# A transformer block on one core: attention scores from two float32r pieces in 48 rows, two heads on the two halves of the array's rows, all maxima from PSUM

## The chip, the core and the metric

The kernel runs on one core of a Trainium2 chip. A core has a matrix engine (TensorE; PE in the profile, PEld for its weight loads), VectorE (DVE), ScalarE (ACT), GpSimd (POOL), and SyncE (SP), which only issues DMAs here. Matrix products go to PSUM, of which the kernel uses eight banks of 512 float32 a partition; DVE and ACT read it; everything else lies in SBUF on 128 partitions. The metric is the time of one execution in microseconds of the device, the median of several runs.

## The reference

One block over 2048 tokens of 512 features, in float32, with 32 heads of 16 features and a feed-forward width of 1792:

```python
mod = (_silu(c) @ w_mod).reshape(c.shape[0], 6, 1, -1)
sa, ca, ga, sb, cb, gb = (mod[:, 0], mod[:, 1], mod[:, 2], mod[:, 3], mod[:, 4], mod[:, 5])
h = _layernorm(x) * (1 + ca) + sa
q, k, v = (h @ wqkv) by head
scores = jnp.einsum("bhqd,bhkd->bhqk", q, k) * Dh ** -0.5
o = jnp.einsum("bhqk,bhkd->bhqd", softmax(scores), v)
x = x + ga * (o @ wo)
h = _layernorm(x) * (1 + cb) + sb
x = x + gb * (_gelu(h @ w1 + b1) @ w2 + b2)
```

The inputs are scaled so that scores are large: the softmax needs the maximum of each row of scores, to float32 accuracy.

## The kernel before, in words

The program has three stages: the projections to q, k and v (with the first layer norm), attention, and the output projection with the feed-forward. The order of instructions on each engine is the order in which the code issues them (a manual schedule); the framework adds the semaphore waits.

Attention works in 32 **units**: a group of four heads (`g`, eight of them) by a block of 512 queries (`qb`, four). A unit has 16 **steps** (`s`), one for each chunk of 128 keys. The scores stand transposed, keys on the partitions and queries in the free dimension.

A score needs float32 accuracy. q and k are split in three bf16 pieces each (in `proj_qk`; ACT, DVE, ACT and POOL make them), and written to DRAM. `build` loads them from there into two stacks, `qst` and `kst`, by 12 DMAs for a group: six products of pieces times 16 features are 96 rows, so that one bf16 matmul gives a float32 score. For three heads of a unit three more rows hold the negative maximum of the query, again in three pieces, against rows of ones in `kst` (99 rows). Their maxima are found ahead: `max_pair` computes scores with the queries on the partitions, 2 x 512 keys into two PSUM banks (`bank_mx`, two such buffers), and DVE takes the maximum of the 1024 (L355, L357), 24 pairs a unit, 34 pairs ahead of the attention at its start (24 and `AHEAD`). `max_rows` joins them, transposes them on PE (L369), copies (L371), splits on POOL (L374, L376), and two DMAs bring them under the queries.

The unit's first head has it otherwise. Its raw scores are computed with a lead of `LEAD` = 20 steps (`raw_chunk`, L393), copied by ACT to a ring of 22 SBUF tiles (L395), and DVE keeps their running maximum (L400). When the unit's 16 chunks are there, `raw_max` transposes the maximum and reduces it (L406, L408), and `raw_spread` sends it to DRAM and back to all partitions (L412 and L414, tiles `x` and `rmaxb`). POOL subtracts it from each tile of the ring (`raw_shift`, L418), and ACT exponentiates in place (L757).

In a step PE computes three scores into a PSUM tile `sc` each (L735, `bank`, three buffers of a bank), ACT exponentiates each (L737), a raw chunk is taken, and parts of the maximum pairs stand between the heads (1.5 pairs a step). Behind them stand the products with v of the step before (`pv_step`, L564): four float32 matmuls of 32 columns each, one for each head, on four quarters of the array's columns. Each float32 matmul is two passes in the trace. The unit's sums gather in one PSUM bank `pv`; at the unit's end ACT copies it (`attn_out`, L550) and eight DMAs store it. The last unit has no maxima to look for; two of its heads then share a wide exponential (L742, L744), and the output projection of the first block stands between its steps (L668).

PSUM: four banks for `mx`, three for `sc`, one for `pv`. Matmuls of the projections and of the feed-forward have float32r operands (128 rows, 512 columns; L286, L668, L809). Pairs and raw chunks that are needed first stand between the matmuls of the last projections (`fill`).

Of the kernel before, what the change touches and what calls it, by code (L numbers as in the profile page):

```python
# [31 lines left out]
RS = 22  # L32
LEAD = RS - 2
# [9 lines left out]
def block_kernel(ctx: ExitStack, tc: tile.TileContext, x, wqkv, wo, w1, b1, w2, b2, c, w_mod, out):  # L43
# [13 lines left out]
    ps_sc = ctx.enter_context(tc.tile_pool(name="ps_sc", bufs=3, space=PSUM))  # L57
# [4 lines left out]

    def bank():
        return ps_sc.tile([P, TB], F32, tag="sc", name="sc")
# [4 lines left out]
    # Rows (part, head in the chunk x d, token); the parts are the three bf16 pieces of a float32.  # L69
    qk_d = [[dram.tile([3, P, S], BF, name=f"qk{w}{k}") for k in range(4)] for w in range(2)]  # L70
# [23 lines left out]
    scm, stx = pool("stx")  # L94

    def stacks(pl):
        return [pl.tile([P, 4, S], BF, name=n) for n in ("qst", "kst")]

    st_x = stacks(stx)
    # The stacks of the even groups lend their space to other data before the first and after the last of them.  # L100
    space = [t.bitcast(F32) for t in st_x]
    halves = [[sp[:, :, :D], sp[:, :, D:]] for sp in space]

# [12 lines left out]
    ones = vwpool.tile([3, S], BF, name="ones")  # L116
# [57 lines left out]
    # silu(c) = c / (1 + exp(-c))  # L174
# [25 lines left out]
    def mod_cols(v, r):  # L200
        """modc[:, v, chunk]: 1 + scale and shift of the feature on the partition"""
# [22 lines left out]
    def ln_stats(tiles):  # L224
        """mean and (var + eps) ** -0.5 of the rows of four tiles"""
# [7 lines left out]
    def transposed(xn, hi, lo, v, pl, bk, engs):  # L233
        """hi + lo of (xn ** T) * (1 + scale) + shift, by feature chunk"""
# [24 lines left out]
    def mx_halves():  # L259
        """the chunks' banks, two to a tile"""  # L260
# [19 lines left out]
    def mm3(ps, ahi, alo, bhi, blo, fill=(), late_b=True):  # L280
        """the three products of a = ahi + alo and b = bhi + blo (alo * blo is below float32's own rounding)"""
# [8 lines left out]
    def proj_qk(b, k, w, fill=()):  # L290
# [32 lines left out]
    st = {}  # L323

    def build(g, t0=0, t1=S):
        q, k = st[g]
        r0 = (g % 2) * 64

        def src(w, parts):
            ap = qk_d[w][g // 2][:, r0 : r0 + 64, t0:t1]  # L330
            return [ap[p].rearrange("(j d) t -> d j t", d=DH) for p in parts]

        for w, dst, parts in ((1, k, (0, 0, 0, 1, 1, 2)), (0, q, (0, 1, 2, 0, 1, 0))):
            for i, ap in enumerate(src(w, parts)):
                sy.dma_start(dst[i * DH : (i + 1) * DH, :, t0:t1], ap)

    def one_rows(k):
        sy.dma_start(k[96:99], one_d[:, None, :].to_broadcast([3, 4, S]))
# [109 lines left out]
    for b in range(NB):  # L448
# [13 lines left out]
        if b == NB - 1:  # L462
            build(0, b * TB, S)
# [446 lines left out]
```

## Time and profile before

| what | us |
|---|---|
| runs: median (lowest to highest, 3 runs) | 2304.33 (2303.45 to 2307.96) |
| span of the profiled execution | 2265.9 |
| first and last pv matmul (the attention stage) | 205.0 and 1905.8 |
| PE busy, share of the span | 2034.7, 90% |
| DVE busy | 1756.7, 78% |
| ACT busy | 1507.4, 67% |
| POOL busy | 1014.6, 45% |
| mean granted TensorE clock, share of full | 0.925 |

The span goes from the first to the last instruction of one profiled execution; the runs' time includes what lies around it. Shares of busy time are means over stages with different limits, and a matmul's recorded time includes its way through the array, so that the starts of two matmuls show what one of them takes in a row. A group of instructions is shown with its source line, engine, operation, tiles, form, count, busy time in all, mean time of one in ns, and the idle time before it with what ended it. A row of a stretch of time is explained where it is shown.

### The profile page before, as it was taken

What the parts mean: (1) busy time and instruction counts of PE and PEld (TensorE: products, weight loads), DVE (VectorE), ACT (ScalarE), POOL (GpSimd) and SP (SyncE); (2) the same over time, 40 slices, a digit from 0 to 9 for tenths busy, and PEclk for the clock granted to TensorE, in tenths of its full rate; (3) what the DMA queues carried; (4) which work ended last, traced back from release to release, by engine and by line L of the source; (5) the groups of instructions that cost most, each with busy time, mean ns of one, the idle gap of its engine ahead of it and who ended that gap; (6) DMA issues with size and microseconds to landing.
All of it is one profiled execution on the core that took longest, in us unless ns stands there. A gap on an engine that the chain in (4) does not pass through costs nothing.

```text
span 2265.9 us, 28250 instructions
## 1 busy us (share of the span) xinstructions
PE 2034.7 (90%) x10202; PEld 855.5 (38%) x10202; DVE 1756.7 (78%) x1819; ACT 1507.4 (67%) x2818; POOL 1014.6 (45%) x890
## 2 busy tenths in 40 slices
PE   8999888888888888888888998888888879999999
PEld 6764222222222222222222222222222224778887
DVE  5288888888888888888888888888888856873653
ACT  3346877777777877777777888777877776222222
POOL 3335454444444444444444444444444554554553
PEclk9999998998888999888889999989999989999999
DMA  6746200400050005001300310050000122532431
GB/s 232 185 152 115 38 18 13 76 8 8 8 76 8 13 8 78 8 8 34 50 8 8 57 27 8 8 76 8 8 13 9 48 81 74 167 116 75 118 115 56
DMA packets 115777, 125.70 MB, mean 55 GB/s; under 512 B 29305, under 2 KB 80537, under 8 KB 115636
## 3 DMA queue, kind: packets, MB, share of 16 engines
q1 hardware_dynamic: 115636, 123.89, 23.5%
q8 instruction: 80, 1.31, 0.3%
q14 instruction: 61, 0.50, 0.1%
HBM read 96.54 MB, written 27.31 MB: 55 GB/s over the span
## 4 chain that ended last, share of the span: by engine, by line
PE 55%; DMA 20%; DVE 12%; issue 4%; ACT 3%; POOL 3%; SPq 0%; ACTq 0%; POOLq 0%; DVEq 0%
PE pv L564 15%; DMA x<-rmax 13%; PE sc L735 10%; PE mx L355 9%; PE sc L286 9%; DMA rmaxb<-x 6%; DVE racc L400 6%; PE mx L809 4%; DVE mxp L357 4%; PE sc L393 3%; POOL ring L418 2%; PE sc L668 2%; PE pv L809 1%; ACT p L737 1%; PE sc L406 1%
## 5 line engine op out<-in xcount | busy, mean ns | idle before, releaser
L357 DVE TENSOR_REDUCE mxp<-mx 128x1 f32<-128x1024 f32 x768 | 921.1, 1218 | 98.2 <-PE mx L355 83.8
L737 ACT ACTIVATE p<-sc 128x512 f32<-128x512 f32 x1488 | 794.5, 598 | 231.2 <-PE sc L735 209.2
L418 POOL TENSOR_TENSOR ring<-ring,rmaxb 128x512 f32<-128x512 f32 x512 | 693.8, 1388 | 479.3 <-DMA rmaxb<-x 479.3
L355 PE MATMUL mx<-kst,qst 96*128 96x512 bf16 x1536 | 621.4, 408 | 1.2 <-DVE mxp L357 1.2
L400 DVE TENSOR_TENSOR racc<-racc,ring 128x512 f32<-128x512 f32 x448 | 509.8, 1138 | 138.4 <-ACT ring L395 137.5
L735 PE MATMUL sc<-qst,kst 99*128 99x512 bf16 x1488 | 609.1, 411 | 6.6 <-DVE r L298 5.5
L564 PE MATMUL pv<-ring,vg 128*32 128x512 f32 x1024 | 577.1, 647 | 10.6 <-ACT osb L550 9.4
L564 PE MATMUL pv<-p,vg 128*32 128x512 f32 x3072 | 583.7, 647 | 0.0
L757 ACT ACTIVATE ring<-ring 128x512 f32<-128x512 f32 x512 | 331.1, 647 | 108.1 <-POOL ring L418 107.9
L735 PEld LDWEIGHTS <-kst 99*128 99x128 bf16 x1488 | 152.4, 103 | 538.9 <-issue 435.3
L395 ACT ACTIVATE ring<-sc 128x512 f32<-128x512 f32 x492 | 301.9, 614 | 12.0 <-PE sc L393 12.0
L393 PE MATMUL sc<-qst,kst 96*128 96x512 bf16 x492 | 199.7, 406 | 99.8 <-ACT p L737 99.6
L374 POOL CAST m<-mr 12x128 bf16<-12x128 f32 x96 | 27.5, 287 | 420.5 <-DVE mr L371 416.4
L355 PEld LDWEIGHTS <-qst 96*128 96x128 bf16 x1536 | 155.8, 103 | 155.4 <-issue 51.6
L564 PEld LDWEIGHTS pv<-ring,vg 128*32 128x32 f32 x1024 | 73.0, 111 | 355.5 <-issue 339.6
L787 ACT ACTIVATE g<-sc,b_c 128x512 f32<-128x512 f32 x56 | 38.6, 690 | 240.4 <-PE sc L286 236.3
L600 POOL TENSOR_TENSOR w1l<-w1r,w1h 128x512 fp32r<-128x512 f32 x56 | 76.7, 1369 | 151.2 <-DVE w1h L599 135.6
L791 DVE TENSOR_TENSOR glo<-g,ghi 128x512 fp32r<-128x512 f32 x56 | 59.3, 1058 | 98.1 <-ACT ghi L790 98.0
L406 PE MATMUL sc<-ident,racc 128*128 128x128 f32 x128 | 28.8, 367 | 95.1 <-DVE racc L400 95.1
L602 POOL TENSOR_TENSOR w2l<-w2r,w2h 128x512 fp32r<-128x512 f32 x56 | 81.2, 1450 | 6.5 <-DVE w2h L601 6.1
L393 PEld LDWEIGHTS <-kst 96*128 96x128 bf16 x512 | 52.7, 103 | 74.7 <-issue 22.9
L564 PEld LDWEIGHTS pv<-p,vg 128*32 128x32 f32 x3072 | 79.8, 111 | 0.0
(145 smaller groups left out, 1898.6 us busy)
## 6 DMA issues: line engine op xcount, KB each, us to landing
w1r<-in_B_w_dram SPq DMA_DIRECT2D x56, 256.0 KB
w2r<-in_B_w_dram SPq DMA_DIRECT2D x56, 256.0 KB
qk<-parts SPq DMA_DIRECT2D x32, 384.0 KB
kst<-qk SPq DMA_DIRECT2D x42, 256.0 KB
qst<-qk SPq DMA_DIRECT2D x42, 256.0 KB
rmaxb<-x SPq DMA_DIRECT2D x32, 256.0 KB
kst<-in_w_mod_dram SPq DMA_DIRECT2D x6, 1024.0 KB
v<-vst SPq DMA_DIRECT2D x8, 664.0 KB
```

Source lines behind the costliest of these rows:

```text
L286: te.matmul(ps, p, q, start=i == 0, stop=i == len(terms) - 1)
L355: ms.append(lambda s=s, k0=k0: te.matmul(ps[:, s], q[:96, j, q0 : q0 + P], k[:96, j, k0 : k0 + TB], start=True, stop=True))
L357: red = lambda: ve.tensor_reduce(mxp[u][:, i : i + 1], ps, axis=AX.XY, op=ALU.max, negate=True)
L393: te.matmul(ps, k[:96, 0, kc * P : (kc + 1) * P], q[:96, 0, qb * TB : (qb + 1) * TB], start=True, stop=True)
L395: ac.activation(sl, ps, AF.Copy)
L400: ve.tensor_tensor(r_acc[u], r_acc[u], sl, op=ALU.max)
L418: gp.tensor_tensor(sl, sl, r_max[c // NKC], op=ALU.subtract)
L564: te.matmul(cur_pv[0][32 * j : 32 * (j + 1)], vg[g][:, kc, j * VW : j * VW + 32], p[:, j - 1] if j else ring[s % RS], start=kc == 0, stop= ...
L735: te.matmul(ps, k[:99, j, kc * P : (kc + 1) * P], q[:99, j, qb * TB : (qb + 1) * TB], start=True, stop=True)
L737: ac.activation(p[:, j - 1], ps, AF.Exp, scale=SCALE)
L757: ac.activation(sl, sl, AF.Exp, scale=SCALE)
L809: te.matmul(acc[qb][t], p[:, sl], q, start=f == 0 and n == 0, stop=f == NF - 1 and n == 2)
```

## The change

q and k are now split in two float32r pieces each (ACT makes the first, DVE the second). Three products of pieces (high x high, low x high, high x low) times 16 features are 48 rows, and two rows more hold the two pieces of the negative maximum against ones: 50 rows (`KR`, `KX`). Two heads of a unit stand on the partitions from 0 and from 64 of the same tile, and the unit's four heads are two such pairs. `kst` is loaded by group (six DMAs, float32 pieces), `qst` by unit (`build_q`: six DMAs, three buffers), in step 2 of the unit two before.

All four heads get their maxima from PSUM: `max_pair` writes 512 keys of two heads to the two banks of `mx`, one matmul on each half of the array's rows, and DVE reduces each bank to its own maximum; there are 32 pairs in a unit, two in a step, behind the second and the fourth head. The ring, the running maximum, its transposes, its two DMAs, POOL's subtraction and the exponential in place are gone.

PSUM is divided anew: `mx` keeps its four banks and `pv` its one; the three others are a double bank `e2` and a single bank `e1`, one buffer each. The heads of all steps go in turn to e2 (two heads, one exponential of 1024) and e1 (one head, one of 512), across the ends of steps: three heads a turn, four heads a step, so the pattern repeats every three steps. In the last unit two heads share a `mx` buffer. `bank`, used by the other stages, takes e1 and the two halves of e2 in turn. Some tiles of the later stages that lent the stacks' space have their own now (`x2a`, `o_b`, `xn_b`).

The diff, cut:

```diff
-RS = 22
-LEAD = RS - 2
+KR = 3 * DH
+KX = KR + 2
+NM = 32
 FILL0 = 3
...
+    ps_e = ctx.enter_context(tc.tile_pool(name="ps_e", bufs=1, space=PSUM))
     ps_pv = ctx.enter_context(tc.tile_pool(name="ps_pv", bufs=1, space=PSUM))
     def bank_mx():
         return ps_mx.tile([P, 2, TB], F32, tag="mx", name="mx")
+    def bank_e2():
+        return ps_e.tile([P, 2, TB], F32, tag="e2", name="e2")
+    def bank_e1():
+        return ps_e.tile([P, TB], F32, tag="e1", name="e1")
+    turn = {"n": 0}
     def bank():
-        return ps_sc.tile([P, TB], F32, tag="sc", name="sc")
+        n = turn["n"] % 3
+        turn["n"] += 1
+        if n == 0:
+            return bank_e1()
+        if n == 1:
+            turn["e2"] = bank_e2()
+        return turn["e2"][:, n - 1]
...
         mm3(ps, [w_hi[k][:, w, i] for i in range(KC)], [w_lo[k][:, w, i] for i in range(KC)],
             [hi[:, i] for i in range(KC)], [lo[:, i] for i in range(KC)], fill)
-        parts = tpool.tile([P, 3, TB], BF, tag="parts", name="parts", bufs=3)
-        r = tpool.tile([P, TB], F32, tag="h32", name="r", bufs=3)
+        parts = tpool.tile([P, 2, TB], FR, tag="parts", name="parts", bufs=3)
         ac.activation(parts[:, 0], ps, AF.Copy)
-        ve.tensor_tensor(r, ps, parts[:, 0], op=ALU.subtract)
+        ve.tensor_tensor(parts[:, 1], ps, parts[:, 0].bitcast(F32), op=ALU.subtract)
         def rest():
-            ac.activation(parts[:, 1], r, AF.Copy)
-            gp.tensor_tensor(parts[:, 2], r, parts[:, 1], op=ALU.subtract)
-            sy.dma_start(qk_d[w][k][:, :, b * TB : (b + 1) * TB].rearrange("a p t -> p a t"), parts)
+            sy.dma_start(qk_d[w][k][:, :, b * TB : (b + 1) * TB].rearrange("a p t -> p a t"), parts.bitcast(F32))
...
+    def heads(w, g, part, a, t0, t1):
         r0 = (g % 2) * 64
-
-        def src(w, parts):
-            ap = qk_d[w][g // 2][:, r0 : r0 + 64, t0:t1]
-            return [ap[p].rearrange("(j d) t -> d j t", d=DH) for p in parts]
-
-        for w, dst, parts in ((1, k, (0, 0, 0, 1, 1, 2)), (0, q, (0, 1, 2, 0, 1, 0))):
-            for i, ap in enumerate(src(w, parts)):
-                sy.dma_start(dst[i * DH : (i + 1) * DH, :, t0:t1], ap)
+        ap = qk_d[w][g // 2][part, r0 : r0 + 64, t0:t1]
+        return ap.rearrange("(p a d) t -> a d p t", a=2, d=DH)[a]
+    def build_k(g, t0=0, t1=S):
+        for i, part in enumerate((0, 0, 1)):
+            for a in range(2):
+                r0 = a * 64 + i * DH
+                sy.dma_start(kst[g][r0 : r0 + DH, :, t0:t1].bitcast(F32), heads(1, g, part, a, t0, t1))
+    def build_q(u):
+        g, qb = divmod(u, NB)
+        qst[u] = kqpool.tile([P, 2, TB], FR, tag="qst", name="qst", bufs=3)
+        for i, part in enumerate((0, 1, 0)):
+            for a in range(2):
+                r0 = a * 64 + i * DH
+                sy.dma_start(qst[u][r0 : r0 + DH].bitcast(F32), heads(0, g, part, a, qb * TB, (qb + 1) * TB))
     def one_rows(k):
-        sy.dma_start(k[96:99], one_d[:, None, :].to_broadcast([3, 4, S]))
+        for a in range(2):
+            r0 = a * 64 + KR
+            sy.dma_start(k[r0 : r0 + 2].bitcast(F32), one_d[:, None, :].to_broadcast([2, 2, S]))
     mxp = {}
-    maxq = [(u, i) for u in range(NG * NB) for i in range(24)]
+    maxq = [(u, i) for u in range(NG * NB) for i in range(NM)]
     mi = [0]
...
     def max_pair(u, i):
-        g, qb = divmod(u, NB)
-        q, k = st[g]
+        g = u // NB
+        q, k = qst[u], kst[g]
         if i == 0:
-            mxp[u] = small.tile([P, 24], F32, tag="mxp", name="mxp")
-        j, qc, kp = 1 + i // 8, (i // 2) % 4, i % 2
+            mxp[u] = small.tile([P, 4, 4, 4], F32, tag="mxp", name="mxp")
+        p, qc, kr = i // 16, (i // 4) % 4, i % 4
         ps = bank_mx()
-        q0 = qb * TB + qc * P
-        ms = []
-        for s in range(2):
-            k0 = (kp * 2 + s) * TB
-            ms.append(lambda s=s, k0=k0: te.matmul(ps[:, s], q[:96, j, q0 : q0 + P], k[:96, j, k0 : k0 + TB],
-                                                    start=True, stop=True))
-        red = lambda: ve.tensor_reduce(mxp[u][:, i : i + 1], ps, axis=AX.XY, op=ALU.max, negate=True)
-        return ms, red
+        for a in range(2):
+            r0 = a * 64
+            te.matmul(ps[:, a], q[r0 : r0 + KR, p, qc * P : (qc + 1) * P], k[r0 : r0 + KR, p, kr * TB : (kr + 1) * TB],
+                      start=True, stop=True)
+        ve.tensor_reduce(mxp[u][:, 2 * p : 2 * p + 2, qc, kr], ps, axis=AX.X, op=ALU.max, negate=True)
...
     def max_rows(u):
-        """-max as three rows of bf16 pieces under the queries"""
-        g, qb = divmod(u, NB)
-        m2 = mxp.pop(u).rearrange("p (r s) -> p r s", s=2)
-        mn = small.tile([P, 12], F32, tag="mn", name="mn")
-        ve.tensor_tensor(mn, m2[:, :, 0], m2[:, :, 1], op=ALU.min)
+        mn = small.tile([P, 16], F32, tag="mn", name="mn")
+        ve.tensor_reduce(mn, mxp.pop(u).rearrange("p h c r -> p (h c) r"), axis=AX.X, op=ALU.min)
         def rest():
-            ps = bank()
-            te.transpose(ps[:12, :P], mn, ident)
-            r = small.tile([12, P], F32, tag="mr", name="mr")
-            ve.tensor_copy(r, ps[:12, :P])
-            m3 = small.tile([12, 3, P], BF, tag="m3", name="m3")
-            for i in range(3):
-                gp.tensor_copy(m3[:, i], r)
-                if i < 2:
-                    gp.tensor_tensor(r, r, m3[:, i], op=ALU.subtract)
-            sy.dma_start(m_d[u].rearrange("a r q -> r a q"), m3)
-            sy.dma_start(st[g][0][96:99, 1:, qb * TB : (qb + 1) * TB], m_d[u].rearrange("a (j c) q -> a j (c q)", j=3))
+            ps = bank_e1()
+            te.transpose(ps[:16, :P], mn, ident)
+            r = small.tile([16, P], F32, tag="mr", name="mr")
+            ve.tensor_copy(r, ps[:16, :P])
+            m2 = small.tile([16, 2, P], FR, tag="m2", name="m2")
+            gp.tensor_copy(m2[:, 0], r)
+            gp.tensor_tensor(m2[:, 1], r, m2[:, 0].bitcast(F32), op=ALU.subtract)
+            sy.dma_start(m_d[u].rearrange("a r q -> r a q"), m2.bitcast(F32))
+            src = m_d[u].rearrange("s (p a c) q -> a s p (c q)", a=2, c=4)
+            for a in range(2):
+                r0 = a * 64 + KR
+                sy.dma_start(qst[u][r0 : r0 + 2].bitcast(F32), src[a])
         return rest
...
+    def next_max():
+        if mi[0] == len(maxq):
+            return []
+        u, i = maxq[mi[0]]
+        mi[0] += 1
+        max_pair(u, i)
+        return [max_rows(u)] if i == NM - 1 else []
...
+        done = 0
+        while mi[0] + done < (NM + AHEAD) * m / nf:
+            fill.append(lambda: new.extend(next_max()))
+            done += 1
         rest = proj_qk(b, k, w, fill)
...
-    mq = []
+    where = {}
+    e1 = 4 * NKC * (NU - 1)
+    e = 0
+    while e < 4 * NS:
+        n = 2 if e >= e1 or (e % 3 == 0 and e + 2 <= e1) else 1
+        for i in range(n):
+            where[e + i] = i, n, bank_mx if e >= e1 else bank_e2 if n == 2 else bank_e1
+        e += n
+    now = {}
+    def exp_step(s, j):
+        u, kc = divmod(s, NKC)
+        q, k = qst[u], kst[u // NB]
+        e = 4 * s + j
+        i, n, bk = where[e]
+        if i == 0:
+            now["ps"] = bk()
+            now["p"] = ppool.tile([P, n, TB], F32, tag=f"p{n}", name="p", bufs=5)
+        ps, pb = now["ps"], now["p"]
+        pt[e] = pb[:, i]
+        p, r0 = j // 2, (j % 2) * 64
+        te.matmul(ps[:, i] if n == 2 else ps, k[r0 : r0 + KX, p, kc * P : (kc + 1) * P], q[r0 : r0 + KX, p],
+                  start=True, stop=True)
+        if i == n - 1:
+            ac.activation(pb if n == 2 else pb[:, 0], ps, AF.Exp, scale=SCALE)
     for s in range(NS):
         u, kc = divmod(s, NKC)
...
-        sl = ring[s % RS]
-        ac.activation(sl, sl, AF.Exp, scale=SCALE)
+        for j in range(4):
+            exp_step(s, j)
+            if j % 2:
+                new += next_max()
         if s:
```

PE in the attention stage, the end of a step before: a head (L735), a maximum matmul (L355), the raw chunk (L393) and pv (L564). A row has the line, the operation, the tiles and the size of the output; in brackets stand the semaphores that it waits for, by the engine that sets them.

```order
L735 LDWEIGHTS kst
L735 MATMUL sc<-qst,kst 128x512 [waits Activation_49]
L355 LDWEIGHTS qst
L355 MATMUL mx<-kst,qst 128x512
L393 LDWEIGHTS kst
L393 MATMUL sc<-qst,kst 128x512 [waits Activation_49]
L564 MATMUL pv<-ring_1019,vg 32x512
L564 MATMUL pv<-p,vg 32x512 x3
```

The same place now, a whole step and the start of the next: heads are L724 (tiles `e_...`: two rows with one number are a double bank), maximum pairs L369, pv L545.

```order
L724 MATMUL e_6270<-qst,kst_820 128x512 [waits Activation_49]
L724 MATMUL e_6270<-qst,kst_820 128x512
L369 MATMUL mx<-kst_1546,qst 128x512 [waits DVE_49]
L369 MATMUL mx<-kst_1546,qst 128x512
L724 MATMUL e_6279<-qst,kst_820 128x512 [waits Activation_49]
L724 MATMUL e_6283<-qst,kst_820 128x512 [waits Activation_49]
L369 MATMUL mx<-kst_1546,qst 128x512 [waits DVE_49]
L369 MATMUL mx<-kst_1546,qst 128x512
L545 MATMUL pv<-p,vg 32x512 x4
L724 MATMUL e_6283<-qst,kst_820 128x512
L724 MATMUL e_6296<-qst,kst_820 128x512 [waits Activation_49]
```

The raw chunk has gone, both matmuls of a pair stand together, and the second half of a double bank can stand behind pv, in the next step. Every first matmul of an e tile waits for ACT, which must have read the tile that had the bank. The weight loads are no rows of their own here, as a float32r matmul brings its own.

ACT in the same stage before: three narrow exponentials (L737), the copy to the ring (L395) and the exponential in the ring (L757).

```order
L737 ACTIVATE p<-sc 128x512 [waits PE_49] x3
L395 ACTIVATE ring_1008<-sc 128x512 [waits PE_49]
L757 ACTIVATE ring_1010<-ring_1010 128x512 [waits Pool_49]
L737 ACTIVATE p<-sc 128x512 [waits PE_49] x3
L395 ACTIVATE ring_1009<-sc 128x512 [waits PE_49]
```

And now (L727):

```order
L727 ACTIVATE p<-e_9409 128x1024 [waits PE_49,Activation_49]
L727 ACTIVATE p<-e_9422 128x512 [waits PE_49]
L727 ACTIVATE p<-e_9430 128x1024 [waits PE_49,Activation_49]
L727 ACTIVATE p<-e_9443 128x512 [waits PE_49]
L727 ACTIVATE p<-e_9447 128x1024 [waits PE_49,Activation_49]
```

Five operations a step have become eight in three steps, a wide and a narrow one in turn, and ACT no longer waits for POOL.

More of the change, by code (lines that the diff above doesn't have):

```diff
@@ L92, in block_kernel @@
     b1_c = const.tile([P, NF], F32, name="b1_c")
[L94 to L102, printed above, removed]
+    lcm, lend = pool("lend")
+    halves = [[lend.tile([P, 4, D], F32, name=f"{n}{i}") for i in range(2)] for n in ("xin", "wmod")]
     tcm, tpool = pool("tpool", bufs=2, side="right")
@@ L380, in max_rows @@
-        return rest
-    raw = {"n": 0}
-    r_acc, r_max = {}, {}
-    def raw_chunk(bk=bank):
-        c = raw["n"]
-        raw["n"] += 1
-        u, kc = divmod(c, NKC)
-        g, qb = divmod(u, NB)
-        q, k = st[g]
-        ps = bk()
-        te.matmul(ps, k[:96, 0, kc * P : (kc + 1) * P], q[:96, 0, qb * TB : (qb + 1) * TB], start=True, stop=True)
-        sl = ring[c % RS]
-        ac.activation(sl, ps, AF.Copy)
-        if kc == 1:
-            r_acc[u] = rpool.tile([P, TB], F32, tag="racc", name="racc")
-            ve.tensor_tensor(r_acc[u], ring[(c - 1) % RS], sl, op=ALU.max)
-        elif kc:
-            ve.tensor_tensor(r_acc[u], r_acc[u], sl, op=ALU.max)
-        return [lambda: [raw_max(u), raw_spread(u)]] if kc == NKC - 1 else []
@@ L403, in raw_max @@
-    def raw_max(u):
-        ps = bank()
-        for t in range(4):
-            te.transpose(ps[:, t * P : (t + 1) * P], r_acc[u][:, t * P : (t + 1) * P], ident)
-        r_max[u] = small.tile([P, 4], F32, tag="rmax", name="rmax")
-        ve.tensor_reduce(r_max[u], ps.rearrange("p (a b) -> p a b", b=P), axis=AX.X, op=ALU.max)
-    def raw_spread(u):
-        sy.dma_start(x_d[u].rearrange("t p -> p t"), r_max.pop(u))
-        r_max[u] = rpool.tile([P, TB], F32, tag="rmaxb", name="rmaxb")
-        sy.dma_start(r_max[u], x_d[u].rearrange("t p -> (t p)")[None, :].to_broadcast([P, TB]))
@@ L483, in block_kernel @@
     rcm, rpool = pool("rpool", bufs=2)
-    ring = [rpool.tile([P, TB], F32, name=f"ring{i}", bufs=1) for i in range(RS)]
     vg = {}
@@ L526, in block_kernel @@
     pcm, ppool = pool("ppool", bufs=2)
-    ycm, sty = pool("sty")
-    st[1] = stacks(sty)
-    one_rows(st[1][1])
-    build(1)
+    kst[1] = ppool.tile([P, 2, S], FR, name="kst1", bufs=1)
+    one_rows(kst[1])
+    build_k(1)
     epool = ctx.enter_context(tc.tile_pool(name="epool", bufs=1, side="right"))
@@ L534, in block_kernel @@
     wo_lo = epool.tile([P, KC, D], FR, name="wo_lo")
+    x2a = [epool.tile([P, 4, D], F32, name=f"x2a{i}") for i in range(2)]
+    o_b = epool.tile([P, 4, D], F32, name="o_b")
+    xn_b = epool.tile([P, 4, D], F32, name="xn_b")
     wo_r = {}
@@ L677, in ln2 @@
         rs = small.tile([P, 4], F32, tag="rs", name="rs")
-        xns[qb] = [halves[0][1][:, t] for t in range(4)]
+        xns[qb] = [xn_b[:, t] for t in range(4)]
         def rows(t):
@@ L703, in block_kernel @@
     base = (NU - 1) * NKC
-    at(base - 8, lambda: load_x2(0, [halves[1][0][:, i] for i in range(4)]))
-    at(base - 7, lambda: load_x2(1, [halves[1][1][:, i] for i in range(4)]))
+    at(base - 8, lambda: load_x2(0, [x2a[0][:, i] for i in range(4)]))
+    at(base - 7, lambda: load_x2(1, [x2a[1][:, i] for i in range(4)]))
     steps = {}
@@ L767, in block_kernel @@
             if g:
[L768 to L769 removed]
+                kst[g + 1] = kst[g - 1]
+                build_k(g + 1)
     pv_step(NS - 1)
[L771 removed]
+    for cm in (pcm, rcm, kqcm):
         close(cm)
```

83 lines of the change are left out of this document (18 added, 65 removed).

## The prediction

> **What bounds the kernel now.** I read the waits first, then a stretch of time inside the attention stage, then single instructions in order of time. The profiled execution has a span of 2265.9 us; the median of the runs shown is 2304.33 us, so 38.4 us lie around the span, and I keep them. The stretches below have their length, then the busy time of PE, PEld, DVE, ACT and POOL, then the granted clock.
>
> ```profile
> 1000.61:1003.23 2.62, 2.62 (x19) 0.76 (x15) 2.57 (x3) 2.58 (x6) 0.00 (x0) 1.00 0.00 0
> 205.00:1850.00 1645.00, 1447.97 (x7539) 416.68 (x7538) 1390.86 (x1296) 1302.98 (x2494) 740.20 (x666) 0.91 0.17 29
> ```
>
> The second row holds 31 of the 32 units (the last is built otherwise): 1645 / 31 = 53.1 us a unit of 16 steps. The first row is one undisturbed step: 2.62 us, PE busy throughout, DVE and ACT at 98%. Sixteen of those are 41.9 us, so 11.2 us of each unit are something else. The waits (total, times, longest) name it.
>
> ```profile
> POOL ring L418 <- DMA rmaxb<-x: 479.3, 31, 16.1
> PE sc L393 <- ACT p L737: 99.6, 31, 5.4
> PE sc L406 <- DVE racc L400: 95.1, 30, 4.4
> 1009.56 1.56 ACT L737 ACTIVATE p<-sc 128x512 f32<-128x512 f32 x3
> 1010.20 0.38 PE L393 MATMUL sc<-qst,kst 96*128 96x512 bf16 x1 [2.85 <-ACT p L737]
> 1011.50 0.61 PE L735 MATMUL sc<-qst,kst 99*128 99x512 bf16 x1
> 1011.90 0.63 PE L355 MATMUL mx<-kst,qst 96*128 96x512 bf16 x1
> ```
>
> Once a unit POOL waits for the first head's maximum to come back by DMA (15.5 us each), ACT then waits for POOL, and PE stands still for some 3 us in two places. Behind such a stop the matmuls run 0.40 us apart, where 0.22 is usual: the granted clock has halved. So the stage has two prices: 2.62 us a step of PE, DVE and ACT alike, and 11.2 us a unit for the round trip of the maximum.
>
> **The change, part by part.** *Removed*: the raw scores, their copies (L395), running maximum (L400), transposes (L406), the two DMAs, POOL's subtraction (L418) and the exponential in place (L757). With them go all three waits above: **11.2 us a unit**. Every engine's load falls too:
>
> ```profile
> L357 DVE TENSOR_REDUCE mxp<-mx 128x1 f32<-128x1024 f32 x768 | 921.1, 1218 | 98.2 <-PE mx L355 83.8
> L737 ACT ACTIVATE p<-sc 128x512 f32<-128x512 f32 x1488 | 794.5, 598 | 231.2 <-PE sc L735 209.2
> L744 ACT ACTIVATE p<-mx 128x1024 f32<-128x1024 f32 x16 | 16.4, 1028 | 11.1 <-PE mx L742 11.1
> ```
>
> DVE gets two reductions a step: 2 x 1.22 = 2.44 us at most. ACT gets 4/3 of a wide and 4/3 of a narrow exponential: 4/3 x (1.03 + 0.60) = 2.17 us. Neither would bound a step above 2.44 us by its own work. What is late next is the path between PE and ACT. Scores now have one bank pair (e2) and one single bank (e1), each held once. Heads go e2, e2, e1, e2, e2, e1 and so on, and PE works in order: a head that waits for its bank holds back the pair of maximum matmuls and the pv group behind it, and so DVE.
>
> *The terms of a step*, from these rows:
>
> ```profile
> 1000.61 0.39 PE L735 MATMUL sc<-qst,kst 99*128 99x512 bf16 x1
> 1001.04 1.58 ACT L737 ACTIVATE p<-sc 128x512 f32<-128x512 f32 x3
> 1001.93 0.38 PE L393 MATMUL sc<-qst,kst 96*128 96x512 bf16 x1
> 1002.24 0.62 PE L564 MATMUL pv<-ring,vg 128*32 128x512 f32 x1
> 1002.25 0.63 PE L564 MATMUL pv<-p,vg 128*32 128x512 f32 x3
> 1002.69 0.59 PE L564 MATMUL pv<-ring,vg 128*32 128x512 f32 x1
> 1877.57 0.59 PE L564 MATMUL pv<-ring,vg 128*32 128x512 f32 x1
> 1878.12 0.19 PEld L668 LDWEIGHTS sc<-wo_lo,p 128*128 128x128 f32 x1 [0.84 <-issue]
> 1878.12 0.50 PE L668 MATMUL sc<-wo_lo,p 128*128 128x512 f32 x1
> 1878.45 0.62 PE L668 MATMUL sc<-wo_hi,p 128*128 128x512 f32 x2
> 2052.01 1.07 PE L286 MATMUL sc<-h2lo,w1h 128*128 128x512 f32 x4
> ```
>
> - ACT starts 0.43 us behind the matmul that fills its bank (1000.61 to 1001.04).
> - A bank comes back 0.05 us after ACT ends: the first of the three at 1009.56 ends at 1010.16, the blocked matmul starts at 1010.20.
> - A float32r matmul of 512 columns takes 0.23 us in a row of them ((1.07 - 0.39) / 3).
> - Its weight load shows when nothing runs in front of it: behind pv the first one lasts 0.50 instead of 0.39 and the next starts 0.33 later instead of 0.23. That is 0.11 us.
> - pv begins 0.31 us behind the last matmul in front of it (0.22 and 0.09 to change over), and its two passes take 0.45 each. The next matmul starts 0.55 behind the second pass: 0.10 to change over.
>
> Does the weight load also show after a wait for a bank? The one blocked pv says so, for its load waited for the bank as the matmul did:
>
> ```profile
> PEld pv L564 <- ACT osb L550: 9.9, 1, 9.9
> PE pv L564 <- ACT osb L550: 9.4, 1, 9.4
> ```
>
> So I charge 0.11 at each hand-back; nothing is the other end.
>
> *Two heads on the two row halves.* No matmul of this trace uses half of the rows, so a pair costs between one matmul (0.23) and two (0.46). The nearest row is pv's, which puts four heads on four quarters of the columns: one at 1002.24, the three others at 1002.25, and all pass in 0.45. I take 0.23. The Trainium skill, "TensorE: Matmul & The Clock Gate", Part 3, has four row tiles give 3.07x instead of 4x; an estimate from that is 1.3 times one matmul, 0.30 us for a pair at most, which would put 0.12 us on the step below and the time at 2295. No run here shows it yet.
>
> *The sum.* The order repeats every three steps. In the first and second, a wide exponential must be done before the last heads can be written: 0.43 + 1.03 + 0.05 + 0.11 = 1.62. Behind it come the pair of maximum matmuls and the change to pv (0.23 + 0.31 = 0.54), pv (0.90), and the way to the first head of the next step (0.10 + 0.11 = 0.21): 3.27 us. In the third step the exponential waited for is a narrow one: 0.43 + 0.60 + 0.05 + 0.11 = 1.19, and the step is 2.84. The mean is **3.13 us**, 0.51 above today's undisturbed step, although every engine has less to do. It also exceeds DVE's 2.44 and ACT's 2.17, so both have gaps.
>
> *Once a unit*: the transposed maxima take the e1 bank, and its next head waits for DVE's copy; osb takes a turn on ACT.
>
> ```profile
> L371 DVE COPY mr<-sc 12x128 f32<-12x128 f32 x32 | 8.7, 272 | 0.1
> L550 ACT ACTIVATE osb<-pv 128x512 f32<-128x512 f32 x32 | 18.5, 580 | 1.2 <-PE pv L564 1.2
> 1009.68 0.32 SPq L552 DMA_DIRECT2D o<-osb  x1
> ```
>
> The copy can stand behind a reduction (1.22 + 0.27), or be hidden wholly by an e2 turn: 0 to 1.5, I take half, 0.75, with 0.05 for osb, which mostly lies beside the change from pv. A unit is 16 x 3.13 + 0.8 = 50.9 us; 31 x (53.1 - 50.9) = **68 us** saved.
>
> *The rest at nothing.* The shifts arrive in time: the maxima are due ten pairs ahead, five steps (15 us), for a transpose, two small POOL operations and two DMAs one behind the other. On SP's queue the six loads of a query block take the place of the former stacks and of the maximum's two DMAs; an issue takes a third of a microsecond (the SPq row above), and their data is due nine steps later. In the projections 42 pairs with two changeovers each could add 42 x (0.09 + 0.10 + 0.11) = 13 us; the end of that stage has this on the chain of waits, and it goes:
>
> ```profile
> 182.17 9.05 DMA x<-rmax
> ```
>
> Fewer bf16 scores there and one piece less per projection pull the same way, so -10 to +10, and I take nothing. The last unit and the feed-forward keep their work.
>
> **Forecast**: 2265.9 - 68 + 38.4 = 2236, rounded to **2235 us**, 3% less.
>
> **Rivals.**
>
> *The halves follow each other* (the other side). Nothing shown runs in half of the rows; if the second matmul starts 0.23 behind the first, steps one and two get 0.46 (a pair of heads and the maximum pair), step three 0.23: on average 0.38, 3.51 a step, 57.0 a unit, 31 x 3.9 = 121 slower: **2425**. It decides from 0.13 us a step, a pair of some 0.31 us. For it: no evidence of overlap in this trace; against it: pv's quarters.
>
> *The weight loads hide.* If PE can load while it waits, 0.11 goes at the hand-back and perhaps 0.11 behind pv: 2.91 to 3.02 a step, 47.4 to 49.1 a unit: **2126 to 2180**. Against it: both rows above.
>
> *The clock halves.* PE now stops for under 1 us, but in every step.
>
> ```profile
> 526.81:530.22 3.41, 1.70 (x11) 0.37 (x11) 0.79 (x2) 3.35 (x7) 3.41 (x4) 1.00 0.12 25
> 530.22:533.64 3.42, 3.42 (x20) 1.14 (x19) 3.20 (x3) 3.42 (x8) 3.42 (x4) 1.00 0.08 18
> 1489.37:1492.78 3.41, 1.62 (x11) 0.36 (x11) 0.74 (x2) 3.28 (x7) 3.41 (x4) 1.00 0.10 23
> 1492.78:1496.20 3.42, 3.42 (x15) 0.82 (x13) 2.33 (x3) 2.79 (x6) 3.42 (x4) 0.50 0.59 182
> ```
>
> A stretch of 3.41 us with 1.70 us of recorded PE work left the clock at 1.00 for the next one; 1.62 halved it. In the new steps PE stands idle between two recorded matmuls for 0.8, 1.0 and 0.3 us while ACT has the bank, 2.1 of 9.4 us, so three quarters are busy, some 2.6 us of 3.41, and I expect full clock. At half clock, with 0.40 a matmul, 0.63 recorded and twice 0.90 for pv, the step is 4.6 us; every second stretch so gives 3.7, 60.4 a unit, **2530**. The Trainium skill, same page, "A second HAM failure mode: psum-queue depth-cycling", says that short idle times between groups while PSUM banks rotate make the clock swing. By that rule this rival would come true; the two rows above speak against it, as the clock held with half a stretch idle.
>
> **How the numbers follow.** The forecast's case has 0.57, with an own range of 2160 to 2320, for the chain has six small terms and 0.1 us a step is 50 us: of it 0.44 faster, 0.05 the same, 0.08 slower. Hidden loads 0.17, faster. Halves in turn 0.19 and the clock 0.07, slower. Together 0.61 faster, 0.05 within 0.2% (about what a measurement of this kernel can tell from no change), 0.34 slower. From 2130 to 2430 only the clock and the tails are left out.
>
> **What would show it.** Right: starts of two row halves under 0.03 us apart; PE idle before each third head, ended by ACT; gaps on DVE and ACT in every step; no POOL work of 1.39 us; units of 51 us with every third step shorter; clock near 1.00. Wrong: halves 0.23 apart; a load that starts before the bank is free; waits that end at DVE's reductions, with steps near 2.44; clock rows at 0.50; a head that waits for its DMA of the shifts.

## The result, and the profile after

| | before | after |
|---|---|---|
| median (lowest to highest), 4 runs each on one chip, us | 2304.93 (2303.45 to 2307.96) | 2245.47 (2242.98 to 2259.84) |
| ratio | | 0.9747 (95%: 0.9717 to 0.9778) |

The change makes the kernel 2.5% faster; 3% was forecast. The profiled execution of after has a span of 2241.2 us and, as a run, took 2242.98, so 1.8 us lie around its span. That is so for every run here whose span is on record, and it is the first surprise: the prediction had kept 38.4 us there.

The stages, read from the first and the last pv matmul of each trace; "before again" is the unchanged kernel profiled once more (experiment e5), and the other rows are the experiments below. The last column is the attention stage, from its first to its last pv matmul, divided by its 32 units. From the first pv matmul of the first unit to that of the last, over the 31 units that are built alike, a unit is 53.52 us in before, 54.83 in before again and 51.18 in after.

| us | first pv | last pv | behind it | span | attention / 32 |
|---|---|---|---|---|---|
| before, the prediction's profile | 205.0 | 1905.8 | 360.2 | 2265.9 | 53.15 |
| before again | 206.1 | 1948.3 | 360.1 | 2308.5 | 54.45 |
| after | 243.1 | 1869.5 | 371.8 | 2241.2 | 50.82 |
| e1, banks apart | 199.8 | 1834.2 | 359.7 | 2194.0 | 51.08 |
| e2, three single banks | 198.7 | 1759.0 | 358.7 | 2117.8 | 45.8 (a later unit) |
| e3, both pairs first | 244.5 | 1759.6 | 371.6 | 2131.2 | 47.35 |
| e4, same half in a row | 262.7 | 3052.3 | 372.8 | 3425.1 | 87.18 |
| e6, before without the ring | 195.0 | 1650.0 | 358.9 | 2008.9 | 45.47 |
| e7, three banks and pairs first | 201.3 | 1550.2 | 359.7 | 1909.9 | 42.15 |
| e8, only the maximum pair on one half | 261.6 | 2911.9 | 372.9 | 3284.8 | 82.82 |

Two of the five runs of e2 (2119.56 us, the profiled one, and 2061.41) had a lower mean clock (0.931 and 0.969) than the three others (0.997 to 0.999, 2015.74 to 2016.58 us); in the profiled one it stood at half for the first 283 us of attention, so the last column has one of its later units, and its ratio rests on the three others.

Against the prediction's own profile, attention got shorter by 1700.8 - 1626.4 = 74.4 us, the stages around it longer by 38.1 + 11.6 = 49.7.

One step of after in the order of time (start, duration, engine, line, operation; in brackets the idle time before it and what ended it):

```profile
1000.03 0.50 PE L724 MATMUL e<-qst,kst 50*128 50x512 f32 x2
1000.37 0.39 PE L369 MATMUL mx<-kst,qst 48*128 48x512 f32 x2
1000.62 1.51 ACT L727 ACTIVATE p<-e 128x1024 f32<-128x1024 f32 x2 [1.81 <-PE e L724]
1000.80 1.23 DVE L371 TENSOR_REDUCE mxp<-mx 128x2 f32<-128x1024 f32 x1 [0.43 <-PE mx L369]
1001.70 0.18 PEld L724 LDWEIGHTS e<-qst,kst 50*128 50x128 f32 x2 [1.37 <-ACT p L727]
1001.70 0.49 PE L724 MATMUL e<-qst,kst 50*128 50x512 f32 x2 [0.94 <-ACT p L727]
1002.03 0.40 PE L369 MATMUL mx<-kst,qst 48*128 48x512 f32 x2
1002.36 1.06 PE L545 MATMUL pv<-p,vg 128*32 128x512 f32 x8
1003.36 0.52 PE L724 MATMUL e<-qst,kst 50*128 50x512 f32 x2
```

The pair of heads at 1000.03 fills the double bank; the pair at 1001.70 needs it again and starts 1.67 us later, when ACT has read it; PE stood idle for 0.94 us until then. From 1000.03 to 1003.36 is one step, 3.33 us. "x2" with a duration of 0.50 says that both row halves start together: a single float32r matmul behind pv had 0.50 as well. All engines have gaps, as the groups of the page say (busy time and mean, then the idle time just before them and what ended it):

```profile
L371 DVE TENSOR_REDUCE mxp<-mx 128x2 f32<-128x1024 f32 x1024 | 1245.7, 1226 | 401.0 <-PE mx L369 398.3
L727 ACT ACTIVATE p<-e 128x1024 f32<-128x1024 f32 (+1 forms) x1323 | 1005.7, 809 | 548.5 <-PE e L724 544.1
L724 PE MATMUL e<-qst,kst 50*128 50x512 f32 x1984 | 633.6, 481 | 313.3 <-ACT p L727 306.8
```

DVE waits 0.39 us before each reduction, almost always for PE; ACT waits for PE, and PE for ACT: nobody is the bound, the hand-over is. The same from 600 to 1200 us (length, then busy PE, PEld, DVE, ACT, POOL with their counts, then the granted clock):

```profile
600.00:1200.00 600.00, 482.45 (x3012) 167.34 (x3010) 462.23 (x400) 386.46 (x513) 8.71 (x24) 1.00 0.13 23
```

PE 80%, DVE 77%, ACT 64%, and a clock of 1.00 all the way. POOL, which had waited 15.5 us a unit for the maximum, has 8.71 us of work left in these 600 us.

The chain of work that ended last says it too, first before, then after (shares of the span by engine):

```profile
PE 55%; DMA 20%; DVE 12%; issue 4%; ACT 3%; POOL 3%; SPq 0%; ACTq 0%; POOLq 0%; DVEq 0%
PE 70%; ACT 21%; issue 4%; DVE 3%; POOL 1%; DMA 1%; SPq 0%; ACTq 0%; POOLq 0%; DVEq 0%
```

DMAs, a fifth of the chain, have all but gone from it (1%), and ACT has taken their place.

The loss before attention shows in the waits of after between 60 and 243 us (engine and line, what it waited for, total, times, longest), in the longest of these in the order of time, and in a stretch:

```profile
PE e L294 <- DVE parts L305: 20.7, 10, 4.6
75.77 1.65 PE L294 MATMUL e<-hThi,w 128*128 128x512 f32 x3 [4.59 <-DVE parts L305]
150.00:175.00 25.00, 21.32 (x80) 13.04 (x80) 14.96 (x15) 3.53 (x7) 2.53 (x2) 0.93 0.26 97
```

A projection (L294) now stands still until DVE's subtraction of an earlier one is done, once for 4.59 us. The last row is a stretch of that stage: 80 matmuls, PE busy for 21.32 of 25 us, a clock of 0.93. Before had 111, a full 25.00 and 1.00 there:

```profile
150.00:175.00 25.00, 25.00 (x111) 16.71 (x110) 24.68 (x26) 10.50 (x20) 7.15 (x7) 1.00 0.32 109
```

### The profile page after: what moved, and what is told of

Its sections match the earlier page's. It is cut to its first block, busy times and chain, and to the rows that moved or that the text cites. A ratio compares the mean times of both kernels' runs of the same rounds, so it can differ in the third digit from the quotient of the medians.

```text
span 2241.2 us, 27287 instructions
## 1 busy us (share of the span) xinstructions
PE 1876.3 (84%) x10586; PEld 884.1 (39%) x10586; DVE 1555.4 (69%) x1563; ACT 1189.5 (53%) x1597; POOL 251.2 (11%) x250
## 4 chain that ended last, share of the span: by engine, by line
PE 70%; ACT 21%; issue 4%; DVE 3%; POOL 1%; DMA 1%; SPq 0%; ACTq 0%; POOLq 0%; DVEq 0%
PE pv L545 22%; PE e L724 21%; ACT p L727 20%; PE e L294 12%; PE mx L369 6%; PE mx L790 4%; PE e L649 2%; PE pv L790 1%; ACT osb L531 1%; DVE mxp L371 1%; PE mx L724 0%; DVE parts L305 0%; POOL w2l L583 0%; DMA rb<-rden 0%; DVE xin L263 0%
## 5 line engine op out<-in xcount | busy, mean ns | idle before, releaser
L371 DVE TENSOR_REDUCE mxp<-mx 128x2 f32<-128x1024 f32 x1024 | 1245.7, 1226 | 401.0 <-PE mx L369 398.3
L727 ACT ACTIVATE p<-e 128x1024 f32<-128x1024 f32 (+1 forms) x1323 | 1005.7, 809 | 548.5 <-PE e L724 544.1
L724 PE MATMUL e<-qst,kst 50*128 50x512 f32 x1984 | 633.6, 481 | 313.3 <-ACT p L727 306.8
L724 PEld LDWEIGHTS e<-qst,kst 50*128 50x128 f32 x1984 | 249.9, 184 | 939.4 <-ACT p L727 778.7
L545 PE MATMUL pv<-p,vg 128*32 128x512 f32 x4096 | 548.9, 607 | 0.0
L369 PE MATMUL mx<-kst,qst 48*128 48x512 f32 x2048 | 528.5, 417 | 0.0
L369 PEld LDWEIGHTS mx<-kst,qst 48*128 48x128 f32 x2048 | 233.4, 187 | 16.7 <-issue 12.3
L545 PEld LDWEIGHTS pv<-p,vg 128*32 128x32 f32 x4096 | 80.9, 108 | 188.6 <-issue 183.1
L294 PE MATMUL e<-hThi,w 128*128 128x512 f32 x256 | 76.8, 447 | 22.6 <-DVE parts L305 19.3
L294 PE MATMUL e<-p,w1h 128*128 128x512 f32 x224 | 75.5, 398 | 3.8 <-ACT h L251 2.2
L790 PE MATMUL mx<-w2h,glo 128*128 128x512 f32 x168 | 66.1, 393 | 3.0 <-DVE glo L772 3.0
L294 PEld LDWEIGHTS e<-hThi,w 128*128 128x128 f32 x256 | 52.2, 213 | 40.7 <-DVE parts L305 22.2
L790 PE MATMUL mx<-w2h,ghi 128*128 128x512 f32 x168 | 65.6, 390 | 0.0
```

The source lines that it names most:

```text
L294: te.matmul(ps, p, q, start=i == 0, stop=i == len(terms) - 1)
L369: te.matmul(ps[:, a], q[r0 : r0 + KR, p, qc * P : (qc + 1) * P], k[r0 : r0 + KR, p, kr * TB : (kr + 1) * TB], start=True, stop=True)
L371: ve.tensor_reduce(mxp[u][:, 2 * p : 2 * p + 2, qc, kr], ps, axis=AX.X, op=ALU.max, negate=True)
L545: te.matmul(cur_pv[0][32 * j : 32 * (j + 1)], vg[g][:, kc, j * VW : j * VW + 32], pt.pop(e), start=kc == 0, stop=kc == NKC - 1)
L724: te.matmul(ps[:, i] if n == 2 else ps, k[r0 : r0 + KX, p, kc * P : (kc + 1) * P], q[r0 : r0 + KX, p], start=True, stop=True)
L727: ac.activation(pb if n == 2 else pb[:, 0], ps, AF.Exp, scale=SCALE)
```

## The experiments

e1 to e4 ran on one chip beside the kernel before (its median 2300.22, 2293.30 to 2307.02), and e5 to e8 on another (before: 2310.27, 2306.38 to 2313.73). Ratios are to that kernel before.

### e1: the former banks outside attention

The pools of PSUM are those of before in the projections and behind attention (three single banks); the double and the single bank exist in attention alone.

```diff
+    scm, ps_sc = pool("ps_sc", bufs=3, space=PSUM)
...
+        if not attn[0] or attn[0] == 3:
+            return ps_sc.tile([P, TB], F32, tag="sc", name="sc")
         n = turn["n"] % 3
...
+    close(scm)
+    ecm, ps_e = pool("ps_e", bufs=1, space=PSUM)
+    attn[0] = 1
```

> Outside attention the three banks are three tiles again; attention has e2 and e1 as in the change. The change's first pv stands at 243 us, where it was 205 before, and its stage after attention takes 372 instead of 360. Theory (the second half of e2 waits until the first half has been read, about 1.8 us at every third projection): nine stops of 1.8 in the last projections and some in the first ones go, 20 to 30 us in all, first pv at 215 to 225. Rival (changeovers between whole-array and half-array matmuls in the fill): nothing goes, first pv stays at 240. Attention's units stay at 51.1 by both.

Measured: 2196.28 (2187.51 to 2197.05), ratio 0.9541 (0.9511 to 0.9570). The first pv matmul came at 199.8 us instead of 243.1 and 359.7 us instead of 371.8 lay behind the last, while the units stayed as they were (51.08 against 50.82). The gain before attention, 43 us, is larger than the 18 to 28 of the expectation (a first pv at 215 to 225). The same stretch of the projections is full again:

```profile
150.00:175.00 25.00, 25.00 (x101) 15.32 (x100) 18.75 (x21) 3.59 (x6) 0.00 (x0) 1.00 0.34 126
```

So both losses outside attention come from the way `bank` hands out e2. A projection takes one half of e2, the next the other; the tile has one buffer, and the second use of the tile waits for every reader of both halves, ACT's copy and DVE's subtraction. With three separate banks no projection's matmul waits for that subtraction, neither in e1 nor before (one weight load does, for 1.0 us). The extra changeovers of the maximum pairs, the prediction's 13 us, are still in e1, yet its first pv is 5 us earlier than before's: on balance the lesser work in that stage covers them.

### e2: three single banks in attention too

Heads take three banks of 512 in turn with an exponential of 512 each; the row halves, the float32r pieces and the maxima stay.

```diff
-    ps_e = ctx.enter_context(tc.tile_pool(name="ps_e", bufs=1, space=PSUM))
+    ps_sc = ctx.enter_context(tc.tile_pool(name="ps_sc", bufs=3, space=PSUM))
...
-        n = 2 if e >= e1 or (e % 3 == 0 and e + 2 <= e1) else 1
+        n = 2 if e >= e1 else 1
```

> All heads take three single banks in turn and narrow exponentials; the other stages have single banks too. Theory (a step is the hand-back of a bank by ACT, the pair of maximum matmuls and pv): the hand-back falls from 1.67 to 1.2 or less and steps become 2.85 alike, units 46.4, 145 us less in attention, with the projections of the first run some 2075 in all. Rival (PE's or DVE's own work, or their changeovers, set the step): steps stay at 3.17. Rival (ACT is the bound and wide exponentials save it time): steps get longer, 4 x 0.49 against 1.87 of ACT.

Measured: 2016.58 (2015.74 to 2119.56); ratio 0.8765 (0.8732 to 0.8798). Each step takes 2.84 us, as expected and the length of the third step of after, and the units 45.8. The time is 58 us below the expected 2075, some 35 of them in attention and the rest outside it, where e1 had already gained more than expected.

```profile
600.00:1200.00 600.00, 553.77 (x3370) 197.73 (x3368) 510.61 (x448) 439.04 (x852) 9.39 (x26) 1.00 0.13 24
```

More exponentials for the same work (852 operations instead of 513 in 600 us), and every engine is busier: PE 92%, DVE 85%. Where a head waits for a bank, it is now always for a narrow exponential. Against e1, which is equal outside attention, this is 2196.28 - 2016.58 = 180 us.

### e3: both maximum pairs behind the second head

```diff
-            if j % 2:
+            if j == 1:
+                new += next_max()
                 new += next_max()
```

> The change with both maximum pairs of a step behind its second head, so that the second pair stands in the wait for the bank and not behind it. Theory: 0.23 us leaves the chain of each step, 2.93 on average, units 47.6, 110 us less than the change: 2135. Rival (DVE hands back the mx buffers too late): the second pair waits for DVE, nothing gained, 2245 or more.

Measured: 2133.20 (2128.11 to 2137.58), ratio 0.9274 (0.9247 to 0.9302). Steps are 3.10, 3.10 and 2.60 instead of 3.33, 3.33 and 2.84. The second pair left the chain for a place where PE waits for ACT anyway. Two pairs in a row also show the price of one:

```profile
1002.10 0.63 PE L369 MATMUL mx<-kst,qst 48*128 48x512 f32 x4
1002.03 0.40 PE L369 MATMUL mx<-kst,qst 48*128 48x512 f32 x2
```

The first row is e3, two pairs; the second after, one pair. 0.63 - 0.40 = 0.23 us for a pair, what one float32r matmul takes in a row of them.

### e4 and e8: halves that cannot run side by side

In e4 the two matmuls of a maximum pair, and two heads in a row, lie on the same half of the rows; in e8 only the maximum pair does.

```diff
-        p, qc, kr = i // 16, (i // 4) % 4, i % 4
+        a, qc, kr = i % 2, (i // 2) % 4, i // 8
         ps = bank_mx()
-        for a in range(2):
-            r0 = a * 64
+        r0 = a * 64
+        for p in range(2):
...
+        j = (0, 2, 1, 3)[j]
```

(The last line is in e4 alone.)

> The change with the same matmuls in another order: the two matmuls that follow each other (two heads, or a maximum pair) are on the same half of the rows, so that they can't run beside each other. Theory (the halves run beside each other in the change, 0.23 a pair): a pair takes 0.46, steps 3.5, units 57, 2245 + 180 = 2425. Rival (each half runs at its own pace whatever stands behind it, or a matmul of half of the rows takes less than 0.23): no more than 2260.

> The change with the two matmuls of each maximum pair on one half of the rows (the halves alternate from pair to pair); the heads stay on both. e4 did this with the heads too, and its clock fell to half for the whole stage. Theory (halves overlap, 0.23 a pair, and 0.46 when a pair is on one half): 0.23 more on the chain of each step, 3.38 to 3.40, units 54.7, 2245 + 112 = 2357, at full clock. Rival (matmuls that fill one half count as half the work for the clock): the clock falls here too, steps of 5 and more, above 2800.

Measured: e4 3425.21 (3423.02 to 3426.92), ratio 1.4892 (1.4855 to 1.4929); e8 3285.52 (3282.59 to 3290.97), ratio 1.4225 (1.4203 to 1.4247). Both miss the price that full clock would have, since the clock stood at half for all of attention up to the last unit, 2754.6 us in e4 and 2618 in e8. The page's row of the clock for e4 (40 slices of the span, in tenths of full), then the stretch from 600 to 1200 us of e4 and of e8, then the first 280 us of attention in the profiled execution of e2:

```profile
PEclk9985555555555555555555555555555555599999
600.00:1200.00 600.00, 587.32 (x1736) 247.46 (x1733) 264.45 (x228) 225.84 (x295) 4.35 (x12) 0.50 0.08 15
600.00:1200.00 600.00, 586.96 (x1826) 236.51 (x1823) 281.48 (x242) 241.10 (x310) 5.09 (x14) 0.50 0.08 15
200.00:480.00 280.00, 280.00 (x1000) 94.97 (x996) 155.84 (x137) 130.52 (x251) 14.34 (x17) 0.50 0.11 20
```

PE is recorded busy for 98% of the time, and yet at half clock. That the order of the halves holds the clock down is not shown. In e2 all pairs lie on two halves, PE was recorded busy for the whole 280 us, and the clock stood at half all the same, before it went up and stayed up. e1 and e7 also went into attention at half clock and left it after 24 and 14 us. Why e4 and e8 did not (their mean clock is 0.59 in every run) stays open. e8's rival named this outcome, steps of 5 and more (measured 5.41, 5.41 and 4.92), but its reason, that a matmul on one half counts as half the work, is not shown either.

What a pair on one half costs at full clock can be seen in the projections, where the clock stood at 1.00 in the stretches below. A maximum pair and the projection matmuls behind it, first in after, then in e8:

```profile
203.13 0.50 PE L369 MATMUL mx<-kst,qst 48*128 48x512 f32 x2
203.56 2.11 PE L294 MATMUL e<-hThi,w 128*128 128x512 f32 x8
218.76 0.73 PE L369 MATMUL mx<-kst,qst 48*128 48x512 f32 x2
219.42 2.09 PE L294 MATMUL e<-hThi,w 128*128 128x512 f32 x8
```

From the pair to the next matmul are 0.43 us in after and 0.66 in e8. The 0.23 more is what one matmul in a row takes, as both expectations had it: halves that differ run side by side, and matmuls on one half take turns. By the sum of e8's expectation that price alone makes 2357; the rest of its 3285.52 came with the clock.

### e5: before again

> The kernel before once more, for its profile. The change's runs last 1.8 us longer than their spans, but the profile of before that the prediction used had a span of 2265.9 beside runs of 2304. Theory (that execution was a shorter one of its kernel, with 1.8 us around it as always): a span of 2290 to 2306 now, 1.8 below the run, and the difference in the attention stage, where the maximum's round trip waits. Rival (some 38 us lie around the span of this kernel): a span near 2266 again.

Measured: 2310.26, with a span of 2308.5. The waits say where this execution differs from the one that the prediction read:

```profile
POOL ring L418 <- DMA rmaxb<-x: 528.9, 31, 18.0
```

479.3 us stood there in the first: 1.6 us more in each unit, and the units are 1.3 us longer. From the last issue of the DMA to DRAM (L412) to POOL's first subtraction it took 13.4 us in the mean there and 14.9 here. So the round trip of the maximum, on which the old units hung, does not take the same time in all executions; whether the chip has a part in it was not tried. The profile shown of before was a short one: all timed runs of before (2293 to 2314 us) are longer, like e5. The time of that execution as a run is not on record, so that 1.8 us lie around it too is taken from the others.

### e6: before, without the ring, in bf16

The other half of the change alone: all four heads get their maxima from PSUM, with the three bf16 pieces, the three single banks and full rows (96 and 99) of before.

```diff
-    maxq = [(u, i) for u in range(NG * NB) for i in range(24)]
+    maxq = [(u, i) for u in range(NG * NB) for i in range(NM)]
...
-        j, qc, kp = 1 + i // 8, (i // 2) % 4, i % 2
+        j, qc, kp = i // 8, (i // 2) % 4, i % 2
...
-                      p[:, j - 1] if j else ring[s % RS], start=kc == 0, stop=kc == NKC - 1)
+                      p[:, j], start=kc == 0, stop=kc == NKC - 1)
...
-        sl = ring[s % RS]
-        ac.activation(sl, sl, AF.Exp, scale=SCALE)
```

> One part of the change alone: no ring, all four maxima from PSUM (32 pairs a unit, two a step), but scores from three bf16 pieces in 96 and 99 rows, three single banks and narrow exponentials as before. Theory (the gain comes from the ring's round trip, and the two pieces with e2 and e1 give part of it back): eight bf16 matmuls of 0.22 and pv with its two changes, 1.09, are 2.84 a step, no hand-back shows, units 46.4, first pv near 200: some 2025, 220 less than the change. Rival (the two pieces and row halves carry the gain): 2245 or more.

Measured: 2016.66 (2010.63 to 2016.88), ratio 0.8730 (0.8715 to 0.8744), the same as e2 within both intervals. PE is the bound here, without a gap:

```profile
600.00:1200.00 600.00, 600.00 (x3382) 181.79 (x3381) 500.17 (x448) 441.30 (x856) 21.82 (x65) 1.00 0.16 24
```

So the gain lies in the ring's removal, which alone gives what e2 gives. The two pieces and row halves, which take PE work away (553.77 us in e2 for the same 448 reductions), do not add to it while the heads hang on the exponentials.

### e7: three single banks, and both pairs first

The edits of e2 and e3 together.

> Three single banks as in e2 and both maximum pairs behind the second head as in e3. Theory: the pair leaves the chain here too, 2.63 a step where e2 had 2.84, units 42.6, some 1915, if the clock stays full; DVE's two reductions (2.44) are close behind. At half clock (e2's first three units, 72 us each) steps take 4.5 and a run gains 26 us for each unit so spent. Rival (DVE's hand-back of the mx buffers binds with shorter steps): 2.84 as in e2, 2016.

Measured: 1903.72 (1901.04 to 1911.64), ratio 0.8246 (0.8226 to 0.8267): the fastest version, 15% below after by the two ratios (0.8246 / 0.9747 = 0.846). Steps take 2.60 us, units 42.15. The expectation, 2.63 us a step and some 1915, came true. The view by stretches has PE at 600 of 600 us, DVE at 91%:

```profile
600.00:1200.00 600.00, 600.00 (x3675) 215.99 (x3671) 544.75 (x488) 478.78 (x929) 10.88 (x30) 1.00 0.14 25
1001.63 0.50 PE L709 MATMUL sc<-qst,kst 50*128 50x512 f32 x2
1004.32 0.49 PE L709 MATMUL sc<-qst,kst 50*128 50x512 f32 x2
1004.66 0.66 PE L354 MATMUL mx<-kst,qst 48*128 48x512 f32 x4
```

Here the two pieces pay: 2.60 us a step against the 2.85 at which PE bounds e6. Whether PE now bounds e7 is not shown: in the same 600 us the heads' weight loads still wait 253.7 us for ACT, in 443 places, beside matmuls that are recorded busy.

## Why the prediction was right, and where it was not

By its own sum, 2265.9 - 68 + 38.4 = 2236, against the profiled run of after, 2265.9 - 74.4 + 49.7 + 1.8 = 2243.0. The attention term was right within 7 us; the two others were wrong by 50 and by 37, in opposite directions. That the total came within 10 us of the median is therefore luck.

- **The chain of a step** was right. Forecast 3.27, 3.27, 2.84; measured 3.33, 3.33, 2.84. The 0.06 sits almost wholly in the first term: the wide exponential starts 0.59 us behind the pair's recorded start, where 0.43 + 0.11 was taken. The 31 units came out at 51.18 instead of 50.9: the steps are 0.04 us longer in the mean, 0.6 a unit, and the transposed maxima cost 0.4 instead of 0.75 (in two units of three a step of 3.33 becomes 3.54, in the third one of 2.84 becomes 3.62). The units of before were misread by as much: the stretch to 1850.00 ends 14 us before the last unit's first pv, at 1864.1, so they are 53.5 and not 53.1. The two slips nearly cancel: 31 x (53.52 - 51.18) = 72.5, and the last unit, 41.7 against 39.8, gives the rest of the 74.4.
- **Why it is a chain** was tested from both sides. e3 takes the pair (0.23) out of it and the units get 3.47 us shorter, 0.22 a step; e2 takes the wide exponential out of it and all steps fall to the 2.84 of the third.
- **The exposed weight load**, 0.11 us at the hand-back, was right: load and matmul both start at 1001.70, as soon as the bank is free, and the next matmul 0.33 us later. The rival in which loads hide did not come.
- **Row halves side by side**, 0.23 us a pair, was right: common starts in after, and the row of four in e3. The Trainium skill ("TensorE: Matmul & The Clock Gate", Part 3) has 3.07x for four row tiles, from which 0.30 had been estimated; for these two halves the trace shows no such loss (0.23 us).
- **The rival in which the halves follow each other** did not come. Its price, 2425, was made at full clock: 0.23 us more for a pair is what e8 shows at full clock, but e4, which builds the rival, took 3425, as its clock fell too.
- **The clock** stayed at 1.00 in the steps, 0.988 over the whole span, though PE stood idle for some 0.94 us in each wide turn. The Trainium skill ("TensorE: Matmul & The Clock Gate", "A second HAM failure mode: psum-queue depth-cycling") tells of a bf16 kernel whose clock swung at short idle times between groups of matmuls. Taken as a rule, that would have had the clock swing here; the trace does not agree, with 1.00 from 600 to 1200 us. The reading that the prediction set against it, that 1.70 us of recorded work in 3.41 us keep the clock and 1.62 halve it, does not carry over either: in the projections of after the clock halved behind a stretch with 1.70 (the granted clock is the third number from the end):

```profile
211.43:214.84 3.41, 1.70 (x8) 1.13 (x7) 2.01 (x3) 0.49 (x1) 0.73 (x2) 1.00 0.19 70
214.84:218.25 3.41, 3.41 (x9) 1.96 (x8) 1.09 (x1) 0.00 (x0) 0.00 (x0) 0.50 0.03 7
```

- **"The rest at nothing" was the step that failed.** Its range of -10 to +10 weighed the changeovers of the maximum pairs between the projections against less work there. The changeovers were priced rightly: a pair stands 0.32 us behind the projection matmul in front of it and 0.43 in front of the next, 0.29 more than two matmuls in a row, 12 us for 42 pairs. With less work beside them, e1's first pv is still 5 us earlier than before's, inside the range. Of the last unit and the feed-forward it said that they "keep their work". They keep their work, but not their banks, since the change rewrote `bank` for all stages: +38.1 us before attention and +11.6 behind it, and e1 gets both back. Of the 43.3 us between after and e1 at the first pv, 20.7 are PE's waits for DVE; the rest came with them, the clock below 1.00 behind such stops among it, and how it divides was not measured.
- **"38.4 us lie around the span" was wrong.** 1.8 us do in every run whose span is on record. The difference between 2265.9 and 2304 was one between two executions, and e5 finds it inside the units. Against e5, attention gained 115.8 us (1742.2 - 1626.4), not 68, and the rest lost 37.0 + 11.7; with the spans that is 2308.5 - 2241.2 = 67.3. A forecast made from the 31 units of e5, 54.83 each, and with 49 us for the banks would have been 2308.5 - 31 x (54.83 - 50.9) + 49 + 2 = 2238.

Where did the rest of a possible gain go? The ring's removal is worth 0.873 by itself (e6); the change returned it through its double bank with one buffer: 180 us in the steps (e1 to e2) and 47 to 49 us outside (after to e1, by spans and by medians). A wide exponential saves ACT 0.17 us against two narrow ones (1.02 against 2 x 0.59), which ACT did not need, and two of the three banks come back only 1.67 us after their matmuls began.

## What to carry to other kernels

When an engine's load falls everywhere, compute the way of one buffer through its producer and consumer next: with as few buffers as here, the hold time of a bank and what stands behind the blocked instruction set the step, so that a narrower operation on more buffers can beat a wider one on fewer. If a shared helper changes, go through all its callers, the stages "not touched" above all. And before a difference between a profile's span and the timed runs is carried along as a constant, compare it with a run of which both are known: it can be one execution against another.

## What the runs showed of the hardware, unexpected

- The clock does not follow the recorded busy time of PE. It was 1.00 with 482 of 600 us busy (after), and 0.50 with 587 of 600 (e4, e8), where the two matmuls of a pair use the same half of the rows, but also with 280 of 280 in e2, where they use different ones. Half clock, once there, can last: e2 left it after 283 us, e4 and e8 only 28 and 30 us after their last maximum pair. What the clock counts instead, and whether e4 and e8 would keep full clock if they once had it in attention, was not tried.
- Two matmuls of 48 or 50 rows on the two halves of the array pass as one: two are recorded in 0.40 us together, where one took 0.39, and the next pair follows 0.23 us later. On the same half the two are recorded in 0.73 us at full clock (e8).
- The round trip of a small result through DRAM took POOL 15.5 us of waiting a unit in one execution and 17.1 in another of the same program (e5).
